# Sliding-window attention maxima taken over 64 queries of two heads at once, from separate copies of q and k in two-slot rings

## The chip, the cores and the metric

The kernel runs on one core of one Trainium2 chip. The metric is the device time of one execution in microseconds (us); shorter is better. TensorE (PE) does the matmuls and loads its stationary operands through a side path (PEld); VectorE (DVE), ScalarE (ACT) and GpSimd (POOL) work beside it; SyncE (SP) issues every DMA transfer, in the order of its queue.

## The reference

Two branches read the same x (2048 rows of 512) and are mixed by a gate per row. All arrays are float32.

```python
qkv = (x @ wqkv).reshape(1, 2048, 3, 32, 16)       # 32 heads of 16
scores = einsum("bhqd,bhkd->bhqk", q, k) * 16 ** -0.5
mask = (i - j >= 0) & (i - j < 256)                # causal, window of 256 keys
a = (softmax(where(mask, scores, -1e9)) @ v) @ wo
b = gelu(x @ w1 + b1) @ w2 + b2                    # 512 -> 1792 -> 512
g = sigmoid((x * gate_w).sum(-1))
out = g * a + (1 - g) * b
```

## The kernel before

Matrix products with weights are split into high and low parts and run as three matmuls each (`mm3`, L89 to L92). Rows are taken in four chunks of T = 512, each of four blocks of 128.

**The program in time.** `qkv(t)` for the four chunks comes first: x is transposed, q, k and v are made, and stored to DRAM (`SQ`, `SK`, `SV`). q and k are stored as two parts (high and low), 16 x 2 rows a head. Then attention runs over 8 groups of four heads, each of 16 blocks, so 128 steps `u`, with pieces of the dense branch (`mlp`, eight turns) between them; then `final`, the product with `wo`. One loop at the end of the function writes the order: at a step it emits, four times over, one matmul for maxima (`att_max`, eight blocks ahead, LEAD = 8), one for scores (`att_exp`), and dense work worth a quarter of STEP = 2296 ns. At every fourth step `att_pvs` multiplies the weights with v for a chunk.

**Maxima and scores.** `att_max` (L382 to L403) multiplies 128 queries of one head with up to 384 keys into a PSUM tile `sm` (three buffers), and DVE adds a mask and takes the row maximum in one instruction (L399), so a block of four heads is four matmuls and four DVE instructions. `att_rows` (L405) waits for four blocks, splits minus the maxima into two parts, transposes them on DVE (L414) and lets POOL copy them as rows into `qs` (`put`, L419). `att_exp` (L424) then gets scores less the maximum out of one matmul over 128 contraction rows; ACT takes the exponential and POOL zeroes the two triangles outside the window.

**Storage.** `qs` holds q for all 2048 queries, 96 rows of parts and 8 rows of maxima; `ks` holds k for all keys, the two heads of a pair interleaved by 64 columns and zeros or ones elsewhere (`clear_k`, L176). Both matmuls read the same two. `load_k` and `att_load` (L348 to L373) refill a chunk of both when its last reader of the group before is done; the third part of a head is the stored high part read once more.

**What sets the order.** PE, ACT, DVE and POOL run in the order in which the program emits their instructions. Work that comes later on other engines is put on a list by `after(ns, ...)` and emitted when a running count (`tick`) passes its due time. SP's queue is ordered by the framework's scheduler, and a transfer that waits holds back all that stand behind it.

**Buffers that the change touches.** Weights come through `raw` (three buffers; each load is split into two parts 10.5 us after it is due, and loads are 4 us apart, LAND and PACE). `h` has eight buffers, for q, k and v on their way to DRAM (L243, L264) and for the seven hidden tiles of an mlp turn. `pt` has 16 (PTS), two a step.

Of the kernel before, what the change touches and what calls it, by code (L numbers as in the profile page):

```python
# [18 lines left out]
T = 512  # L19
# [13 lines left out]
def gated_mix(ctx: ExitStack, tc: tile.TileContext, x, wqkv, wo, w1, b1, w2, b2, gate_w, out):  # L33
# [11 lines left out]
    def f32(ap):  # L45
# [6 lines left out]
    SQ = [dr.tile([H, 16, 2, T], F32, name=f"SQ{t}") for t in range(NT)]  # L52
    SK = dr.tile([H, 16, 2, S], F32, name="SK")
# [13 lines left out]
    mask = cp.tile([128, 384], BF16, name="mask")  # L67
    nc.gpsimd.memset(mask, 0.0)
    nc.gpsimd.affine_select(out=mask[:, 0:128], in_=mask[:, 0:128], pattern=[[1, 128]],
                            compare_op=ALU.is_ge, fill=NEG, base=-1, channel_multiplier=-1)  # L70
    nc.gpsimd.affine_select(out=mask[:, 256:384], in_=mask[:, 256:384], pattern=[[-1, 128]],
                            compare_op=ALU.is_ge, fill=NEG, base=0, channel_multiplier=1)
# [5 lines left out]
    for k in (0, 1):  # L78
        nc.gpsimd.affine_select(out=own[96:104], in_=own[96:104], pattern=[[-2, 4]], compare_op=ALU.not_equal,
                                fill=1.0, base=-k, channel_multiplier=1)  # L80
    nms = cp.tile([128, RB, 32], F32R, name="nm")
# [39 lines left out]
    def load_raw(key, early=False):  # L121
# [6 lines left out]
        if early and kind == "v":  # L128
            if i == 0:
                raws["v"] = f32(sb.tile([128, NC, 2, T], F32R, tag="xt", bufs=1, name="raw_v"))  # L130
            raw = raws["v"][:, i, 0]
        elif early:
            raw = sb.tile([128, 2, 320], F32, tag="pt", bufs=PTS, name=f"raw_{kind}{i}")
            raw = raw.rearrange("p a b -> p (a b)")[:, 0:T]
        else:
            raw = sb.tile([128, T], F32, tag="raw", bufs=3, name=f"raw_{kind}{i}")
# [32 lines left out]
    ks = cp.tile([128, 2, 2 * S], F32R, name="ks")  # L169
# [6 lines left out]
    def clear_k(i):  # L176

        pr, n = divmod(i, 4)
        for s in range(2):
            v = of_head(ks[:, pr, n * 1024:(n + 1) * 1024], s)  # L180
            nc.scalar.activation(v, nil.unsqueeze(2).unsqueeze(3).broadcast_to([128, 4, 2, 64]), AF.Identity,
                                 bias=own[:, 2 * pr + s:2 * pr + s + 1])

    xts, xrs = {}, {}

    def load_xr(t):
        for b in range(NB):
            xrs[t, b] = sb.tile([128, D], F32, tag=("tmp", "raw")[b // 3], bufs=3, name=f"xr{t}_{b}")
            nc.sync.dma_start(xrs[t, b], x[t * T + b * 128:t * T + (b + 1) * 128])

    def qkv_x(t, b):

        if b == 0:
            if t < NT - 1:
                v = (ks[:, 0], ks[:, 1], qs.rearrange("p a c -> p (a c)"))[t]
# [38 lines left out]
    def qkv_qk(t, j):  # L234
# [8 lines left out]
        e = sb.tile([128, 2, T], F32R, tag="h", bufs=8, name=f"qke{t}_{j}")  # L243
# [6 lines left out]
        def lo():  # L250
            nc.vector.tensor_sub(e[:, 1 - h], p, f32(e[:, h]))  # L251
            nc.sync.dma_start(dst[8 * i:8 * i + 8].rearrange("h d s c -> (h d) s c"), f32(e))
# [3 lines left out]
    def qkv_v(t, b):  # L256
# [7 lines left out]
        vx = f32(sb.tile([128, 2, T], F32R, tag="h", bufs=8, name=f"vx{t}_{b}"))  # L264
# [19 lines left out]
    def qkv(t):  # L284
# [17 lines left out]
        for n, (kind, j) in enumerate(pieces):  # L302
# [17 lines left out]
            if t == 2 and n in (1, 3, 5, 7):  # L320
                clear_k(4 + n // 2)
            if t == 2 and n in (2, 4):
                load_k(0, n // 2 - 1, slice(0, 1))
            if t == 2 and n in (9, 10):
                load_k(0, n - 9, slice(1, 2))
# [22 lines left out]
    def load_k(g_, c, prs):  # L348
# [3 lines left out]
        for pr in range(prs.start, prs.stop):  # L352
            for s in range(2):
                src = SK[4 * g_ + 2 * pr + s]
                for r, n, part in ((32 * s, 32, src.rearrange("d u c -> (d u) c")), (64 + 16 * s, 16, src[:, 0])):
                    v = f32(ks[r:r + n, pr])
                    k0, m = (c * T, NB) if s == 0 else (c * T - 64, NB) if c else (64, NB - 1)
                    to = v[:, 2 * k0 + 64:2 * k0 + 64 + 256 * m] if s else v[:, 2 * k0:2 * k0 + 256 * m]
                    to = to.rearrange("r (n x) -> r n x", x=256)
                    to = to[:, :, 0:128] if s else to[:, :, 64:192]  # L360
                    nc.sync.dma_start(to, part[:, k0:k0 + 128 * m].rearrange("r (n x) -> r n x", x=128))
                    if s and c == 0:
                        nc.sync.dma_start(v[:, 0:64], part[:, 0:64])
                    if s and c == NT - 1:
                        nc.sync.dma_start(v[:, 2 * S - 64:2 * S], part[:, S - 64:S])

    def att_load(g_, c, q_only=False):
        need(("qk", c, g_ // 2))
        if not q_only:
            load_k(g_, c, slice(0, 2))  # L370
        src, to = SQ[c][4 * g_:4 * g_ + 4], f32(qs[:, :, c * T:(c + 1) * T])
        nc.sync.dma_start(to[0:64], src.rearrange("(a s) d u c -> (s d u) a c", a=2))
        nc.sync.dma_start(to[64:96], src[:, :, 1].rearrange("(a s) d c -> (s d) a c", a=2))  # L373
# [11 lines left out]
    def att_max(g_, b, i):  # L385

        if b % RB == 0 and (g_, b // RB) not in Ms:
            Ms[g_, b // RB] = sb.tile([128, RB, 4], F32, tag="M", bufs=2, name=f"M{g_}_{b}")
        M = Ms[g_, b // RB]
        k0 = max(b - 2, 0) * 128  # L390
        w = (b + 1) * 128 - k0
        pr, s = divmod(i, 2)
        p = ps.tile([128, 384], F32, tag="sm", bufs=3, name=f"sm{g_}_{b}_{i}")
        nc.tensor.matmul(p[:, :w], qs[0:96, pr, b * 128:(b + 1) * 128], of_head(ks[0:96, pr, 2 * k0:2 * (k0 + w)], s),  # L394
                         start=True, stop=True)
        junk = sb.tile([128, 384], BF16, tag="jm", bufs=1, name=f"jm{g_}_{b}_{i}")

        def red():
            nc.vector.tensor_tensor_reduce(junk[:, :w], p[:, :w], mask[:, 384 - w:384], 1.0, -3e38,  # L399
                                           ALU.add, ALU.max, M[:, b % RB, i:i + 1])  # L400
# [4 lines left out]
    def att_rows(g_, rb):  # L405
# [3 lines left out]
        nm = nms[:, :, 0:8].rearrange("p b (i k) -> p k b i", k=2)  # L409
# [3 lines left out]
        tt = sb.tile([128, RB, 32], F32, tag="tt", bufs=1, name=f"tt{g_}_{rb}")  # L413
        nc.vector.transpose(tt.rearrange("p b c -> p (b c)"), f32(nms).rearrange("p b c -> p (b c)"))  # L414

        def put(i):
            dst = qs[96:104, :, rb * RB * 128:(rb + 1) * RB * 128]
            dst = dst.rearrange("r s (b i j) -> r s b i j", b=RB, i=4)[:, :, :, i]
            nc.gpsimd.tensor_copy(dst, tt[32 * i:32 * i + 8].unsqueeze(1).broadcast_to([8, 2, RB, 32]))  # L419
# [5 lines left out]
    def att_exp(g_, kb, i):  # L425
# [9 lines left out]
        nc.tensor.matmul(p[:, :w], ks[:, pr, 2 * k0:2 * k0 + 128], qs[:, pr, k0:k0 + w],  # L435
# [99 lines left out]
    def load_o(t, cs=range(NC)):  # L535

        if ("o", t) not in xts:
# [3 lines left out]
            else:  # L541
                xts["o", t] = [sb.tile([128, 2, T], F32R, tag="h", bufs=8, name=f"ot{t}_{c}") for c in range(NC)]
        ot = xts["o", t]
        for c in cs:
            need(("o", t, c))
            if t == 0:
                raw = sb.tile([128, T], F32, tag=("x1", "raw")[c % 2], bufs=2 + c % 2, name=f"or{t}_{c}")
# [60 lines left out]
    def mlp(n):  # L608
# [6 lines left out]
        for i in range(HF):  # L615
# [7 lines left out]
            h = sb.tile([128, 2, T], F32R, tag="h", bufs=8, name=f"h{t}_{f}")  # L623
# [48 lines left out]
    def load_y(t):  # L672

        need(*[("y", 1, t, b) for b in range(NB)])
        for i in range(NB // 2):
            v = f32(ks[:, i, 2 * t * T:2 * (t + 1) * T]).rearrange("p (j f) -> p j f", j=2)
# [67 lines left out]
    chunks = [divmod(i, NT) for i in range(NG * NT)]  # L744
    fill(START - AHEAD)
    need(("v", NT - 2, NB - 1))
    att_load(*chunks.pop(0), True), att_load(*chunks.pop(0), True)
    fill(AHEAD)
    for u in range(-LEAD, NU):
# [15 lines left out]
        if m % NB == LPOS and m > 0 and chunks:  # L765
            att_load(*chunks.pop(0))
        if u % NB == 0 and u >= 0:
            att_load_v(*divmod(u // NB, NT))
        if u >= NU - NKB + NB and u % NB == 1:
            load_y((u % NKB) // NB - 1)  # L770
# [8 lines left out]
LPOS = 0  # L779
LASTN = 2  # L780
WARM = (7, 3)
RB = 4
NKB = S // 128
PTS = 16
# [36 lines left out]
```

## Time and profile before

| quantity | value |
|---|---|
| time, median of 3 runs | 769.8 us (769.8 to 769.93) |
| the profiled execution's own time | 769.51 us |
| its span, first to last instruction | 767.8 us |
| granted TensorE clock | 1.00 |
| PE busy | 748.8 us, 98% |
| DVE, ACT, POOL busy | 534.1, 432.6, 385.9 us |
| moved by DMA | 137.81 MB, DMA engines busy 59.4% on the main queue |

The span lies 1.7 us under the profiled time. Shares over the whole span mix stages: the first 130 us are projections, then come attention and the dense branch together, and the last 50 us are the dense tail. A matmul's printed duration holds the time to fill and drain the array, which overlaps with its neighbours; the distance between the starts of two neighbours is what it takes from PE.

### The profile page before, as it was taken

The page shows a single profiled execution, that of the slowest core. Times are in us where ns is not written, and L with a number is a line of the kernel's source. Part 1 is how long each engine was busy: PE and PEld are TensorE (multiplying, and loading weights), DVE is VectorE, ACT ScalarE, POOL GpSimd, SP SyncE. Part 2 cuts the span into 40 slices and gives each one's busy share as a digit, 9 for nine tenths or more (in the row PEclk, how much of TensorE's full clock was granted, in tenths as well). Part 3 has the DMA queues.
Part 4 walks back from the last instruction along what each step waited for, and adds up shares of the span by engine and source line. Part 5 has one row for each costly group of instructions (what it writes and reads, how often), then busy time and mean ns, then how long its engine had stood idle before and what let it go on. Part 6 is the DMA issues. An engine that isn't in the chain of part 4 may idle for free.

```text
span 767.8 us, 18330 instructions
## 1 busy us (share of the span) xinstructions
PE 748.8 (98%) x6102; PEld 614.3 (80%) x6102; DVE 534.1 (70%) x1548; ACT 432.6 (56%) x945; POOL 385.9 (50%) x1125
## 2 busy tenths in 40 slices
PE   8999999988999999999999999999999999999998
PEld 6888888866888888788877877888888788878786
DVE  4532332889669868976897798679878886893553
ACT  4434433358458646754885587448646763785641
POOL 2200000018666765766567677658765775777200
PEclk9999999999999999999999999999999999999999
DMA  9986856765643565575345756653575474436583
GB/s 299 358 296 203 319 182 219 252 195 166 179 119 73 181 196 138 142 209 151 95 114 156 212 163 193 185 126 94 172 206 158 107 214 125 132 107 200 171 261 110
DMA packets 136558, 137.81 MB, mean 179 GB/s; under 512 B 53264, under 2 KB 88592, under 8 KB 136464
## 3 DMA queue, kind: packets, MB, share of 16 engines
q1 hardware_dynamic: 136464, 136.64, 59.4%
q8 instruction: 49, 0.80, 0.4%
q14 instruction: 45, 0.37, 0.2%
HBM read 82.58 MB, written 54.00 MB: 178 GB/s over the span
## 4 chain that ended last, share of the span: by engine, by line
PE 84%; DVE 8%; issue 3%; ACT 3%; DMA 1%; SPq 1%; POOL 0%; DVEq 0%; POOLq 0%; ACTq 0%
PE sm L394 10%; PE st L435 8%; PE pv_sm L472 7%; PE y L90 7%; PE y L91 6%; PE y L92 6%; PE u L90 5%; PE u L91 5%; PE u L92 5%; PE qk L92 4%; DVE jm L399 4%; PE qk L90 4%; PE qk L91 4%; PE a L90 2%; PE v L92 2%
## 5 line engine op out<-in xcount | busy, mean ns | idle before, releaser
L399 DVE CUSTOM_DVE_ANT_0 jm<-sm,mask 128x384 bf16<-128x384 f32 (+2 forms) x512 | 269.6, 527 | 66.8 <-PE sm L394 38.8
L450 ACT ACTIVATE pt<-st 128x320 f32<-128x320 f32 (+4 forms) x512 | 206.1, 421 | 134.1 <-PE st L435 129.4
L441 POOL TENSOR_SCALAR_AFFINE_SELECT pt<-pt 64x128 f32<-64x128 f32 x512 | 176.5, 345 | 184.8 <-ACT pt L450 166.1
L394 PE MATMUL sm<-ks,qs 96*128 96x384 f32 (+2 forms) x512 | 171.7, 338 | 10.7 <-DVE M L399 9.0
L435 PE MATMUL st<-qs,ks 128*128 128x320 f32 (+4 forms) x512 | 155.0, 305 | 0.7 <-ACT pt L450 0.7
L444 POOL TENSOR_SCALAR_AFFINE_SELECT pt<-pt 64x128 f32<-64x128 f32 x448 | 154.7, 345 | 0.0
L394 PEld LDWEIGHTS sm<-ks,qs 96*128 96x128 f32 x512 | 96.2, 188 | 44.1 <-DVE M L399 21.1
L435 PEld LDWEIGHTS st<-qs,ks 128*128 128x128 f32 x512 | 97.3, 190 | 18.3 <-ACT pt L450 1.1
L90 PE MATMUL y<-w,h 128*128 128x512 f32 x224 | 90.1, 402 | 0.0
L91 PE MATMUL y<-w,h 128*128 128x512 f32 x224 | 88.4, 395 | 0.0
L92 PE MATMUL y<-w,h 128*128 128x512 f32 x224 | 87.8, 392 | 0.0
L419 POOL CAST qs<-tt 8x256 fp32r<-8x256 f32 x128 | 62.3, 487 | 47.2 <-PE u L92 37.9
L90 PE MATMUL u<-mx,w 128*128 128x512 f32 x196 | 80.4, 410 | 0.0
L91 PE MATMUL u<-mx,w 128*128 128x512 f32 x196 | 77.3, 395 | 0.0
L92 PE MATMUL u<-mx,w 128*128 128x512 f32 x196 | 76.8, 392 | 0.0
L472 PE MATMUL pv_st<-pt,vbuf 64*32 64x320 f32 (+4 forms) x1408 | 73.1, 346 | 0.8 <-POOL pt L441 0.8
L472 PE MATMUL pv_sm<-pt,vbuf 64*32 64x320 f32 (+4 forms) x1408 | 73.4, 346 | 0.1
L472 PEld LDWEIGHTS pv_sm<-pt,vbuf 64*32 64x32 f32 x1408 | 49.9, 106 | 19.9 <-issue 2.1
L251 DVE TENSOR_TENSOR qke<-qk,qke 128x512 fp32r<-128x512 f32 x32 | 22.1, 690 | 48.9 <-ACT qke L248 40.5
L248 ACT ACTIVATE qke<-qk 128x512 fp32r<-128x512 f32 x32 | 19.1, 598 | 56.0 <-PE qk L92 37.1
L92 PEld LDWEIGHTS y<-w,h 128*128 128x128 f32 x224 | 42.1, 188 | 9.7
L496 DVE TENSOR_TENSOR nd<-nd,pv_sm 128x512 f32<-128x512 f32 x32 | 21.9, 684 | 39.0 <-ACT nd L493 38.8
(124 smaller groups left out, 1337.6 us busy)
## 6 DMA issues: line engine op xcount, KB each, us to landing
mx<-XT SPq DMA_DIRECT2D x24, 512.0 KB
SQ<-qke SPq DMA_DIRECT2D x16, 512.0 KB
SK<-qke SPq DMA_DIRECT2D x16, 512.0 KB
qs<-SQ SPq DMA_DIRECT2D x32, 256.0 KB
ND<-nd SPq DMA_DIRECT2D x32, 256.0 KB
ks<-SK SPq DMA_DIRECT2D x112, 64.0 KB
raw_w<-in_B_w_dram SPq DMA_DIRECT2D x28, 256.0 KB
SV<-vx SPq DMA_DIRECT2D x16, 272.0 KB
```

Source lines behind the costliest of these rows:

```text
L90: nc.tensor.matmul(p, lh, rh, start=first, stop=False)
L91: nc.tensor.matmul(p, lh, rl, start=False, stop=False)
L92: nc.tensor.matmul(p, ll, rh, start=False, stop=last)
L251: nc.vector.tensor_sub(e[:, 1 - h], p, f32(e[:, h]))
L394: nc.tensor.matmul(p[:, :w], qs[0:96, pr, b * 128:(b + 1) * 128], of_head(ks[0:96, pr, 2 * k0:2 * (k0 + w)], s), start=True, stop=True)
L399: nc.vector.tensor_tensor_reduce(junk[:, :w], p[:, :w], mask[:, 384 - w:384], 1.0, -3e38, ALU.add, ALU.max, M[:, b % RB, i:i + 1])
L419: nc.gpsimd.tensor_copy(dst, tt[32 * i:32 * i + 8].unsqueeze(1).broadcast_to([8, 2, RB, 32]))
L435: nc.tensor.matmul(p[:, :w], ks[:, pr, 2 * k0:2 * k0 + 128], qs[:, pr, k0:k0 + w], start=True, stop=True)
L441: nc.gpsimd.affine_select(out=v[:, :, 0:64], in_=v[:, :, 0:64], pattern=[[0, 2], [1, 64]], compare_op=ALU.is_ge, fill=0.0, base=0, channel ...
L444: nc.gpsimd.affine_select(out=v[:, :, W:W + 64], in_=v[:, :, W:W + 64], pattern=[[0, 2], [-1, 64]], compare_op=ALU.is_ge, fill=0.0, base=- ...
L450: nc.scalar.activation(pt[:, pr, :w], p[:, :w], AF.Exp, scale=SCALE)
L472: nc.tensor.matmul(pv[r // 64][32 * i:32 * i + 32, q - c * T:e - c * T], vts[g_, b // NB][r:r + 64, v:v + 32], rhs(r), start=start, stop=s ...
```

## The change

`att_max` now takes 64 queries of both heads of a pair at once. The queries lie in a new tile `qd`, block-diagonal: head 0's 64 queries in rows 0 to 47, head 1's in rows 48 to 95, zeros elsewhere. The keys lie in a new tile `kd`, both heads' parts one above the other, without interleaving. 64 queries see at most 320 keys. A block is still four matmuls and four DVE instructions, over 320 columns for 384. `qd`, `kd` and `ks` are rings of two chunk slots; `qs` stays whole. The rows of minus the maxima move to rows 0 to 3 and 64 to 67 of `qs`, four partitions of 512 elements where there were eight of 256. q and k are stored with three parts a head, the third by a transfer of its own. `h` goes from 8 buffers to 7, `raw` from 3 to 2, `pt` from 16 to 14; weight loads before 150 us of the program's count are staged in `pt`.

```diff
-    SQ = [dr.tile([H, 16, 2, T], F32, name=f"SQ{t}") for t in range(NT)]
-    SK = dr.tile([H, 16, 2, S], F32, name="SK")
+    SQ = [dr.tile([H, 16, 3, T], F32, name=f"SQ{t}") for t in range(NT)]
+    SK = dr.tile([H, 16, 3, S], F32, name="SK")
...
-    nms = cp.tile([128, RB, 32], F32R, name="nm")
+    nms = cp.tile([128, 2 * RB, 32], F32R, name="nm")
...
-    ks = cp.tile([128, 2, 2 * S], F32R, name="ks")
+    ks = cp.tile([128, 2, 2, 2 * T], F32R, name="ks")
+    qd = cp.tile([128, 2, 2, 2 * T], F32R, name="qd")
+    kd = cp.tile([128, 2, 2, W + T], F32R, name="kd")
...
-            nc.sync.dma_start(dst[8 * i:8 * i + 8].rearrange("h d s c -> (h d) s c"), f32(e))
+            to = dst[8 * i:8 * i + 8].rearrange("h d s c -> (h d) s c")
+            nc.sync.dma_start(to[:, 0:2], f32(e))
+            nc.sync.dma_start(to[:, 2], f32(e[:, h]))
...
+    def load_ks(g_, c):
+        need(("qk", c, NC + g_ // 2))
+        src = parts(SK, g_, slice(c * T, (c + 1) * T))
+        for pr in range(2):
+            for s in range(2):
+                v = f32(ks[64 * s + 4:64 * s + 52, pr, slot(g_, c)]).rearrange("r (n u j) -> r n u j", u=4, j=64)
+                w = src[s, :, pr].rearrange("r (n u j) -> r n u j", u=2, j=64)
+                if s:
+                    nc.sync.dma_start(v[:, :, 0], w[:, :, 0])
+                    nc.sync.dma_start(v[:, :, 3], w[:, :, 1])
+                else:
+                    nc.sync.dma_start(v[:, :, 1:3], w)
+    def load_kd(g_, c):
+        need(("qk", c, NC + g_ // 2))
+        k0 = max(c * T - W, 0)
+        src = SK[4 * g_:4 * g_ + 4, :, :, k0:(c + 1) * T].rearrange("(a s) d u c -> (s d u) a c", s=2)
+        nc.sync.dma_start(f32(kd[0:96, :, slot(g_, c), k0 - c * T + W:]), src)
+    def load_qd(g_, c):
...
+                v = f32(qd[48 * s:48 * s + 48, pr, slot(g_, c)]).rearrange("r (n s j) -> r n s j", s=2, j=64)[:, :, s]
+                nc.sync.dma_start(v, src[s, :, pr].rearrange("r (n j) -> r n j", j=64))
+    def load_qs(g_, c):
...
+            nc.sync.dma_start(f32(qs[64 * s + 4:64 * s + 52, :, c * T:(c + 1) * T]), src[s])
...
-        k0 = max(b - 2, 0) * 128
-        w = (b + 1) * 128 - k0
-        nc.tensor.matmul(p[:, :w], qs[0:96, pr, b * 128:(b + 1) * 128], of_head(ks[0:96, pr, 2 * k0:2 * (k0 + w)], s),
+        hb, pr = divmod(i, 2)
+        w = min(64 * (2 * b + hb + 1), W + 64)
+        k1 = 64 * (j + 1) + W
+        nc.tensor.matmul(p[:, :w], qd[0:96, pr, n, 128 * j:128 * (j + 1)], kd[0:96, pr, n, k1 - w:k1],
...
+            r = 64 * (i // 2)
+            dst = qs[r:r + 4, :, rb * RB * 128:(rb + 1) * RB * 128]
+            nc.gpsimd.tensor_copy(dst, tt[32 * i:32 * i + 4].unsqueeze(1).broadcast_to([4, 2, 2 * RB, 32]))
...
-        if m % NB == LPOS and m > 0 and chunks:
-            att_load(*chunks.pop(0))
+        if m in range(1, NT + 1):
+            load_qs(0, m - 1)
+        if m % NB == 0 and 0 < m < NU - NB:
+            load_qd(*divmod(m // NB + 1, NT)), load_kd(*divmod(m // NB + 1, NT))
+        if u % NB == 1 and NB < u < NU - NB:
+            load_ks(*divmod(u // NB + 1, NT))
+        if u % NB == 2 and NB < u < NU - 3 * NB:
+            load_qs(*divmod(u // NB + 3, NT))
```

On PE the instructions stand in the same order as before, one for one. What moves is SP's queue. At the end of the third chunk of the first group of heads SP's rows before were these (`nd` is a chunk's result of attention, `vbuf` holds v):

```order
L361 DMA ks<-SK 32x4x128
L361 DMA ks<-SK 16x4x128 x2
L372 DMA qs<-SQ_72 64x2x512
L373 DMA qs<-SQ_72 32x2x512
L380 DMA vbuf<-SV_78 128x4x34
L382 DMA vbuf<-SV_78 64x4x34
L497 DMA ND_0_95<-nd_2_2529 128x512
L382 DMA vbuf<-SV_78 64x4x34
```

And with the change, at the same place:

```order
L395 DMA qd<-SQ_72 48x8x64 x3
L529 DMA ND_0_95<-nd_2_2565 128x512
L395 DMA qd<-SQ_72 48x8x64
L387 DMA kd<-SK 96x2x768
L408 DMA vbuf<-SV_78 128x4x34
L410 DMA vbuf<-SV_78 64x4x34 x2
L381 DMA ks<-SK 48x4x128
L378 DMA ks<-SK 48x4x64
L379 DMA ks<-SK 48x4x64
L381 DMA ks<-SK 48x4x128
L378 DMA ks<-SK 48x4x64
L379 DMA ks<-SK 48x4x64
```

The four transfers of `qd` and the one of `kd` now stand at the head of a chunk, around the store of `nd`; v follows, then the six of `ks`, and behind these rows the two of `qs`.

On POOL the copies of the maxima (`CAST`) keep their place between the two triangle selections of a block. Before and after, at the second chunk's first block:

```order
L444 AFFINE_SELECT pt_4_0_1886<-pt_4_0_1886 64x2x64
L419 CAST qs<-tt_2_1896 8x2x4x32 x3
L441 AFFINE_SELECT pt_4_1_1909<-pt_4_1_1909 64x2x64
```

```order
L476 AFFINE_SELECT pt_4_0_1919<-pt_4_0_1919 64x2x64
L450 CAST qs<-tt_2_1930 4x2x8x32 x3
L473 AFFINE_SELECT pt_4_1_1943<-pt_4_1_1943 64x2x64
```

Only their shape changed.

124 lines of the change are left out of this document (62 added, 62 removed).

## The prediction

> **What bounds the kernel now.** First the page's busy times and the granted clock, then the matmuls in time, then what PE waits for, then the stretches.
>
> ```profile
> PE 748.8 (98%) x6102; PEld 614.3 (80%) x6102; DVE 534.1 (70%) x1548; ACT 432.6 (56%) x945; POOL 385.9 (50%) x1125
> PEclk9999999999999999999999999999999999999999
> ```
>
> PE is busy for 98% at full clock, so in most of the span each column that a matmul does not stream is time. The groups by shape give durations; a piece of PE's timeline (start, duration) gives the price of a column:
>
> ```profile
> L394 PE MATMUL sm<-ks,qs 96*128 96x384 f32 x448 | 155.5, 350 | 10.7 <-DVE M L399 9.0 <-DVE nd L496 1.2
> L394 PE MATMUL sm<-ks,qs 96*128 96x256 f32 x32 | 9.0, 282 | 0.0
> L394 PE MATMUL sm<-ks,qs 96*128 96x128 f32 x32 | 7.3, 228 | 0.0
> L435 PE MATMUL st<-qs,ks 128*128 128x320 f32 x448 | 139.9, 314 | 0.7 <-ACT pt L450 0.7
> ...
> 208.10 0.40 PE L90 MATMUL y<-w,h 128*128 128x512 f32 x1
> 208.33 0.39 PE L91 MATMUL y<-w,h 128*128 128x512 f32 x1
> 208.56 0.39 PE L92 MATMUL y<-w,h 128*128 128x512 f32 x1
> 208.79 0.28 PE L394 MATMUL sm<-ks,qs 96*128 96x256 f32 x1
> 208.91 0.31 PE L435 MATMUL st<-qs,ks 128*128 128x320 f32 x1
> 209.06 0.28 PE L394 MATMUL sm<-ks,qs 96*128 96x256 f32 x1
> ```
>
> Starts are 0.23 us apart behind 512 columns, 0.12 behind 256, 0.15 behind 320: 0.45 to 0.47 ns a column, the weight loads hidden. Next, everything that PE stood idle for, with the longest single wait last in each row:
>
> ```profile
> PE sm L394 <- DVE M L399: 9.0, 17, 1.2
> PE warm0.0_177 L281 <- POOL idle L49: 1.3, 1, 1.3
> PE sm L394 <- DVE nd L496: 1.2, 3, 0.5
> PE pv_st L472 <- POOL pt L441: 0.8, 1, 0.8
> PE pv_sm L472 <- DVE M L399: 0.8, 3, 0.3
> PE st L435 <- ACT pt L450: 0.7, 1, 0.7
> PE qk L90 <- ACT qk L145: 0.7, 1, 0.7
> PE u L90 <- ACT sqh L572: 0.3, 1, 0.3
> ```
>
> No transfer is in this list: PE waits for no DMA. What it does wait for is DVE, which is late in emptying the three `sm` buffers. The stretches say where (length, then PE, PEld, DVE, ACT and POOL busy, clock, DMA share, GB/s):
>
> ```profile
> 20.00:40.00 20.00, 20.00 (x97) 16.53 (x97) 9.81 (x18) 9.47 (x20) 4.71 (x7) 1.00 0.95 341
> ...
> 160.00:190.00 30.00, 24.78 (x171) 18.23 (x170) 26.34 (x74) 21.95 (x46) 17.85 (x43) 1.00 0.62 202
> 190.00:700.00 510.00, 502.68 (x4749) 414.92 (x4749) 408.66 (x1262) 319.60 (x718) 343.06 (x1005) 1.00 0.55 152
> ```
>
> At the start of attention (160 to 190) PE loses 5.2 us and DVE is 88% busy; over the 510 us behind it PE loses 7.3 us.
>
> **The maxima on PE.** The count of matmuls stays. Of the 512, 448 go from 384 to 320 columns; of the 32 of a group's second block, half go from 256 to 192; of the 32 of its first, half go from 128 to 64. That is 480 matmuls of 64 columns less. At 0.45 ns a column, 29 ns each, the sum is **13.9 us**. Bounds: the mean durations 350 and 314 differ by 36 ns, 17 us; the gap of 0.03 us between 256 and 320 columns in the timeline, read at its rounding (20 ns), 10 us. The order on PE does not move and the stationary operand stays 96 by 128, so no load is added. I take 13.9, since the spacing is what PE pays.
>
> **The maxima on DVE.**
>
> ```profile
> L399 DVE CUSTOM_DVE_ANT_0 jm<-sm,mask 128x384 bf16<-128x384 f32 x448 | 247.1, 551 | 54.3 <-PE sm L394 29.4 <-PE st L435 0.3
> L399 DVE CUSTOM_DVE_ANT_0 jm<-sm,mask 128x256 bf16<-128x256 f32 x32 | 13.6, 424 | 8.6 <-PE sm L394 7.1
> L414 DVE STREAM_TRANSPOSE tt<-nm 128x128 f32<-128x128 f32 x32 | 10.0, 311 | 4.0 <-DVE nm L411 0.5 <-POOL pt L444 0.5
> L419 POOL CAST qs<-tt 8x256 fp32r<-8x256 f32 x128 | 62.3, 487 | 47.2 <-PE u L92 37.9 <-DVE tt L414 2.6
> ```
>
> 551 less 424 over 128 columns is 0.99 ns a column, so 64 columns are 64 ns, and 480 of them 30.5 us of DVE. The transpose of twice the columns costs between nothing and another 311 ns; at the same 0.99 ns a column 127 ns, 4.1 us in 32 (at most 10). DVE thus gives back 26 us, most of it while PE is busy anyway. What counts is the backlog: a block asks 4 x 64 ns less of DVE (0.03 us of that spent on transposes) and 4 x 29 ns less of PE, so DVE gains 0.11 us a block on PE. If DVE sets the pace in half of the 128 blocks (the gelu halves), that is 7 us; PE's visible waits on DVE (9.0 + 1.2) are the ceiling, 0 the floor. I take **4.5 us** off, a little under the middle, since part of the backlog comes from DVE standing behind `nd`, which the change leaves.
>
> **POOL.** The 128 copies keep their bytes but run over 512 elements in 4 partitions where there were 256 in 8: between 487 ns and twice that; if a POOL instruction goes by elements, nearer the upper end, 0 to 62 us in all and up to 2 us a chunk. POOL is busy 343 of 510 us in attention, and no row above is a wait for these copies. Scores first need them two steps later, and what stands behind them on POOL is the selections of a chunk just begun, which `pv` reads a chunk later. Cover gone, 2 us in each of 32 chunks would be exposed. I cost it at nothing.
>
> **Transfers.**
>
> ```profile
> DMA packets 136558, 137.81 MB, mean 179 GB/s; under 512 B 53264, under 2 KB 88592, under 8 KB 136464
> q1 hardware_dynamic: 136464, 136.64, 59.4%
> ...
> 300.67 2.73 SPq L361 DMA_DIRECT2D ks<-SK  x5
> ...
> 311.91 1.29 SPq L382 DMA_DIRECT2D vbuf<-SV  x2
> ...
> 331.42 1.72 SPq L382 DMA_DIRECT2D vbuf<-SV  x2
> ...
> SPq L361 <- PE st L435: 65.7, 53, 6.1
> SPq L137 <- DVE w L149: 24.6, 16, 4.1
> ```
>
> Projections: the third part of q and k adds 32 stores of 256 KB, 8.4 MB; at 341 GB/s for a share of 0.95, the rate of the stretch from 20 to 40 us, 23 us of all engines over some 150 us. PE was 100% busy in that stretch with DMA at 0.95, so that close a queue does not reach it. The x rows are the reader nearest by; in SP's queue of the first chunk they stand no later than before. Nothing.
>
> Attention: a chunk reads `qd` 384 KB, `kd` 576 KB (96 rows, two pairs, 768 columns), `ks` and `qs` 384 KB each; before, only the last two. That is 0.98 MB more, 2.7 us of all engines by bytes at the rate above. By packets: `qd` in rows of 64 columns has 1536, `ks` 1152 for 768, `kd` 192, 2112 more; at the mean packet of 53 ns (59.4% of 16 x 767.8 us over 136464), 7.0 us. A chunk lasts 19.5 us (the two `vbuf` rows), so the share goes from 0.55 to between 0.69 and 0.91. The Trainium skill's page "DMA: Bandwidth & Descriptors", section Specifications, speaks against the change: transfers in pieces under 512 B do a read-modify-write. Were the 256-byte rows of `qd` and half of `ks`, 576 KB, to count twice, a chunk would take an estimated 1.6 us more than by bytes, still within the bound by packets; no row of this run isolates it.
>
> Lateness: a chunk has 16 issues (4 `qd`, 1 `kd`, 3 v, 6 `ks`, 2 `qs`). Five `ks` took 2.73 us, 0.55 each, so 8.8 us; then 1.8 MB to land, 5.3 us by bytes. Together 14 of 19.5 us, and the ring slot is free as the chunk begins, so SP loses most of the 65.7 us for which it waited on scores. I cost it at nothing; the cover is 5 us, and the longest hold of SP before was 6.1.
>
> Smaller pools: with two `raw` buffers a load must wait for the one two before it, due 8 us earlier, which DVE frees some 12 us after its time (LAND plus the split). So a load starts 4 us late and has about 6.5 us to land before ACT wants it. Where SP is held, ACT, and behind it the exponentials, stand for a few us, at 14 paced loads at most. Between 0 and 6 us; **1.5 us** on. With 7 `h` and 14 `pt` the next use follows the last reader in the program's order, and I add nothing.
>
> Sum against the profiled execution: 769.5 - 13.9 - 4.5 + 1.5 = 752.6. Its time lies 0.3 us under the median, so **753 us**.
>
> **Rivals.**
>
> 1. *The rings starve PE (slower).* `ks` is loaded behind `qd`, `kd` and v, and at a chunk's first score PE stands until it lands. Against it: 14 of 19.5 us, and nothing waited for DMA before. For it: the share may reach 0.91, and one hold of SP eats the cover. It decides once issue and landing pass 19.5 us; at 1 us over in each of 28 chunks 753 + 28 = 781 us.
> 2. *The staging of weights.* ACT waits at most loads through `raw`, the full 6 us in place of 1.5: 757, and with the DVE relief gone too, 762.
> 3. *DVE gives nothing back.* The transposes stand in front of maxima and cost the full 311 ns, and the backlog behind `nd` stays: 769.5 - 13.9 + 1.5, 757.
> 4. *The copies on POOL come late.* 2 us a chunk are exposed at the scores: 753 + 64, or 785 at half. For it only the doubled length.
> 5. *The columns saved are not PE's time.* DVE sets the pace throughout and gives less than it saves: no change, 769. Against it: PE loses 7.3 of 510 us.
>
> **How the numbers follow.** Forecast 0.64; rival 1 0.09, 2 0.11, 3 0.10, 4 0.03, 5 0.03. The likeliest is 753; with its own bounds (10 to 17 on PE, 0 to 10 on DVE) it spans 744 to 761. The range takes in rivals 2 and 3 as well and leaves out 1, 4 and 5, 0.15 in all: 745 to 763. A measurement can tell about 0.2% from no change. Faster 0.85 (forecast, 2, 3), within 0.2% 0.03 (5), slower 0.12 (1, 4).
>
> **What would show it.** `sm` matmuls of 320 columns at 314 ns, starts 0.15 us apart, x448; the DVE instruction at 487 ns; PE's waits on `M` under 9.0 us; PE still at 97% or more. PE's list without DMA and without `qs` copies. A row `sm <- DMA kd` or `st <- DMA ks` of many us would be rival 1, `ACT w <- DMA raw_w` rival 2, `st <- POOL qs` rival 4. DVE at 508 us, POOL up by as much as 62 us and the DMA share at 0.69 to 0.91 would bear out the bounds.

## The result, and the profile after

The changed kernel takes **805.7 us** (median of 4 runs, 802.71 to 806.79) against 769.8 before: a ratio of 1.046, interval 1.0432 to 1.0489. It is 36 us slower; 753 was predicted. The profiled execution took 806.2 us, its span is 804.5. Of all the executions used below, one, of the version with three slots of `ks`, ran in a slower state (892.66 us at a granted clock of 0.754) and is in no ratio.

The page of the changed kernel, busy times, then the transfers:

```profile
PE 755.9 (94%) x6102; PEld 616.2 (77%) x6102; DVE 510.1 (63%) x1548; ACT 432.8 (54%) x941; POOL 422.7 (53%) x1129
...
DMA packets 208494, 176.09 MB, mean 219 GB/s; under 512 B 126480, under 2 KB 150288, under 8 KB 208400
...
q1 hardware_dynamic: 208400, 174.91, 78.6%
```

PE is no longer busy for 98% of the span, and though it streams 480 x 64 columns less, its busy time went up by 7 us: the matmuls themselves took longer, at a mean granted clock of 0.975 for 1.00. Packets rose by half. What PE waited for (sum, times, longest), then what SP's queue waited for:

```profile
PE st L467 <- DMA ks<-SK: 19.6, 14, 3.7
PE sm L424 <- DMA kd<-SK: 10.3, 4, 6.5
PE sm L424 <- DVE M L429: 2.4, 7, 0.5
```

```profile
SPq L529 <- DVE nd L528: 43.3, 15, 4.8
...
SPq L378 <- DMA kd<-SK: 18.0, 15, 2.3
...
SPq L549 <- DMA RD<-den: 14.6, 6, 6.0
```

The list that held no transfer before is now led by two. SP, which had waited for scores, now waits most for what it has to store (`nd`, made on DVE) and for its own earlier transfers to land: 15 times a `ks` of one head stood until `kd` had landed. The wait for the `sm` buffers, the only real one before, shrank from 9.0 to 2.4 us. The stretches of attention (length, then PE, PEld, DVE, ACT and POOL busy, clock, DMA share, GB/s):

```profile
160.00:190.00 30.00, 22.46 (x121) 18.38 (x127) 23.57 (x68) 21.01 (x46) 15.52 (x32) 0.89 0.79 200
190.00:700.00 510.00, 477.88 (x4514) 389.95 (x4499) 361.66 (x1199) 295.29 (x662) 350.52 (x945) 0.97 0.79 198
```

Over the 510 us PE now loses 32 (7.3 before), at a clock of 0.97 for 1.00. The DMA share went from 0.55 to 0.79, but the rate from 152 to 198 GB/s: share grew by 44%, bytes by 30%.

**The first stop.** The chain of work that ended last, PE's timeline, and the stretches around it, 5 us each:

```profile
153.02 8.74 DMA SK<-qke
161.77 8.35 DMA kd<-SK
```

```profile
170.25 0.60 PE L424 MATMUL sm<-kd,qd 96*128 96x320 f32 x1 [6.53 <-DMA kd<-SK]
```

```profile
160.00:165.00 5.00, 3.58 (x16) 2.39 (x14) 3.95 (x12) 2.83 (x5) 0.00 (x0) 1.00 1.20 262
165.00:170.00 5.00, 0.00 (x0) 0.00 (x0) 1.10 (x3) 1.78 (x3) 0.00 (x0) 0.72 1.07 249
170.00:175.00 5.00, 4.75 (x15) 4.09 (x16) 3.96 (x13) 2.38 (x6) 1.39 (x4) 0.60 1.00 174
175.00:180.00 5.00, 4.62 (x24) 3.76 (x22) 4.86 (x13) 4.95 (x11) 4.70 (x9) 1.00 0.02 7
```

The store of k takes 8.7 us, `kd`, which reads it, another 8.4, with the DMA engines full; PE stands for 6.5 us. Behind the stop the matmuls run at a granted clock of 0.60 over 5 us. So the stop costs more than its own length.

**A stop at the scores.** SP's timeline ahead of one, PE's waits, and the stretches of 4 us:

```profile
441.54 0.57 SPq L395 DMA_DIRECT2D qd<-SQ  x1
442.56 0.62 SPq L549 DMA_DIRECT2D num<-ND  x1
446.11 0.61 SPq L549 DMA_DIRECT2D rb<-RD  x1
446.81 0.41 SPq L529 DMA_DIRECT2D ND<-nd  x1
447.27 1.94 SPq L395 DMA_DIRECT2D qd<-SQ  x3
449.25 1.18 SPq L387 DMA_DIRECT2D kd<-SK  x1
...
453.89 0.43 SPq L381 DMA_DIRECT2D ks<-SK  x1
456.04 0.32 SPq L378 DMA_DIRECT2D ks<-SK  x1
...
457.86 0.44 SPq L379 DMA_DIRECT2D ks<-SK  x1
```

```profile
456.16 0.39 PE L424 MATMUL sm<-kd,qd 96*128 96x320 f32 x1 [0.85 <-DMA kd<-SK]
459.72 0.61 PE L467 MATMUL st<-qs,ks 128*128 128x320 f32 x1 [3.17 <-DMA ks<-SK]
```

```profile
452.00:456.00 4.00, 3.12 (x14) 1.80 (x12) 3.57 (x13) 2.29 (x6) 1.74 (x6) 1.00 1.00 233
456.00:460.00 4.00, 0.67 (x2) 0.50 (x3) 0.33 (x2) 0.69 (x1) 0.00 (x0) 0.67 0.80 229
460.00:464.00 4.00, 4.00 (x21) 3.09 (x28) 3.13 (x11) 1.93 (x5) 1.26 (x3) 0.50 0.92 241
```

From the store of `nd` to the score that waited are 12.9 us, much like the 14 us of the prediction. One of the four `qd` went out at 441.5. The rest of the row starts only with the store at 446.8, 9.7 us before PE wants `ks` (459.72 less 3.17): the loads of the normalisation (`num`, `rb`) and the store, all ahead in the queue, held it. It is the same at all seven stops of over 1 us for `ks` (1.06 to 3.72 us): the store of `nd` went out 8.7 to 13.3 us before PE wanted `ks`. The DMA engines are at 1.00 with 233 GB/s, not the 341 that the estimate used.

**The clock.** At 460 to 464 the granted clock is 0.50. Two more stretches of 4 us, the first at the end of a stop of 2.01 us of the changed kernel, the second behind one of 3.76 us in a run below (narrow maxima with the old transfers):

```profile
668.00:672.00 4.00, 3.41 (x10) 2.90 (x11) 0.92 (x3) 0.88 (x2) 0.81 (x4) 0.62 0.92 215
```

```profile
332.00:336.00 4.00, 4.00 (x13) 3.52 (x12) 2.47 (x9) 1.31 (x3) 1.49 (x6) 0.50 0.18 41
```

The second has the DMA engines nearly idle (0.18), while the clock was 1.00 at 160 to 165 and at 452 to 456 with shares of 1.20 and 1.00: the low clock goes with the stop and not with the traffic. In the changed kernel the clock falls below 0.9 in eight places, seven of them at a stop of PE of 2.01 us or more, one at two of 1.06 and 0.82 us with one matmul between; four single stops of 1.06 to 1.65 us left it at 1.00. The Trainium skill's page "TensorE: Matmul & The Clock Gate", section "HAM oscillation — how this bites in real kernels", gives the rule that PE should have no idle gap of more than about 3.4 us, behind which it is throttled to half its clock. The trace agrees on the half (0.50) but not on the length: here a gap of 2.01 us was enough.

The groups by shape:

```profile
L429 DVE CUSTOM_DVE_ANT_0 jm<-sm,mask 128x320 bf16<-128x320 f32 x448 | 217.0, 484 | 68.6 <-PE sm L424 46.5
...
L424 PE MATMUL sm<-kd,qd 96*128 96x320 f32 x448 | 142.6, 321 | 14.0 <-DMA kd<-SK 10.3 <-DVE M L429 2.4 <-DVE nd L528 0.7
...
L450 POOL CAST qs<-tt 4x512 fp32r<-4x512 f32 x128 | 90.2, 705 | 46.2 <-DVE tt L444 38.9
L444 DVE STREAM_TRANSPOSE tt<-nm 128x256 f32<-128x256 f32 x32 | 14.3, 445 | 3.3
```

The engines' own costs came out as forecast: the maximum 484 ns (487), the matmul 321 (314), the transpose 445 (311 + 127), the copy 705, between its bounds of 487 and 974.

### The profile page after: what moved, and what is told of

Same layout as the page of the kernel before. It is cut to its first block, busy times and chain, and to the rows that moved or that the text cites. A ratio compares the mean times of both kernels' runs of the same rounds, so it can differ in the third digit from the quotient of the medians.

```text
span 804.5 us, 18387 instructions
## 1 busy us (share of the span) xinstructions
PE 755.9 (94%) x6102; PEld 616.2 (77%) x6102; DVE 510.1 (63%) x1548; ACT 432.8 (54%) x941; POOL 422.7 (53%) x1129
## 2 busy tenths in 40 slices
DMA packets 208494, 176.09 MB, mean 219 GB/s; under 512 B 126480, under 2 KB 150288, under 8 KB 208400
## 3 DMA queue, kind: packets, MB, share of 16 engines
q1 hardware_dynamic: 208400, 174.91, 78.6%
## 4 chain that ended last, share of the span: by engine, by line
PE 68%; DMA 20%; DVE 5%; issue 2%; SPq 2%; POOL 1%; ACT 1%; DVEq 0%; POOLq 0%
PE pv_sm L504 7%; PE st L467 6%; PE sm L424 6%; DMA ks<-SK 6%; PE u L93 5%; PE u L95 4%; PE u L94 4%; DMA kd<-SK 4%; PE y L93 4%; PE qk L93 4%; PE qk L95 4%; PE qk L94 4%; PE y L94 4%; PE y L95 4%; DMA qd<-SQ 2%
## 5 line engine op out<-in xcount | busy, mean ns | idle before, releaser
L429 DVE CUSTOM_DVE_ANT_0 jm<-sm,mask 128x320 bf16<-128x320 f32 (+4 forms) x512 | 237.5, 464 | 91.5 <-PE sm L424 67.1
L473 POOL TENSOR_SCALAR_AFFINE_SELECT pt<-pt 64x128 f32<-64x128 f32 x512 | 186.7, 365 | 178.3 <-ACT pt L482 157.1
L467 PE MATMUL st<-qs,ks 128*128 128x320 f32 (+4 forms) x512 | 159.5, 315 | 21.3 <-DMA ks<-SK 19.6
L424 PE MATMUL sm<-kd,qd 96*128 96x320 f32 (+4 forms) x512 | 158.2, 311 | 14.5 <-DMA kd<-SK 10.3
L476 POOL TENSOR_SCALAR_AFFINE_SELECT pt<-pt 64x128 f32<-64x128 f32 x448 | 152.4, 340 | 0.0
L424 PEld LDWEIGHTS sm<-kd,qd 96*128 96x128 f32 x512 | 98.0, 191 | 43.1 <-DVE M L429 13.5
L450 POOL CAST qs<-tt 4x512 fp32r<-4x512 f32 x128 | 90.2, 705 | 46.2 <-DVE tt L444 38.9
L95 PE MATMUL y<-w,h 128*128 128x512 f32 x224 | 89.7, 400 | 1.7 <-DVE h L619 1.7
L93 PE MATMUL y<-w,h 128*128 128x512 f32 x224 | 91.1, 407 | 0.0
L94 PE MATMUL y<-w,h 128*128 128x512 f32 x224 | 89.8, 401 | 0.0
L504 PE MATMUL pv_sm<-pt,vbuf 64*32 64x320 f32 (+4 forms) x1408 | 77.5, 358 | 2.8 <-DVE M L429 2.4
L504 PE MATMUL pv_st<-pt,vbuf 64*32 64x320 f32 (+4 forms) x1408 | 77.0, 358 | 0.6 <-POOL pt L473 0.6
L504 PEld LDWEIGHTS pv_st<-pt,vbuf 64*32 64x32 f32 x1408 | 49.0, 110 | 0.9 <-POOL pt L473 0.9
```

The lines of the kernel that those rows point to most:

```text
L93: nc.tensor.matmul(p, lh, rh, start=first, stop=False)
L94: nc.tensor.matmul(p, lh, rl, start=False, stop=False)
L95: nc.tensor.matmul(p, ll, rh, start=False, stop=last)
L424: nc.tensor.matmul(p[:, :w], qd[0:96, pr, n, 128 * j:128 * (j + 1)], kd[0:96, pr, n, k1 - w:k1], start=True, stop=True)
L450: nc.gpsimd.tensor_copy(dst, tt[32 * i:32 * i + 4].unsqueeze(1).broadcast_to([4, 2, 2 * RB, 32]))
L467: nc.tensor.matmul(p[:, :w], ks[:, pr, slot(g_, kb // NB), at:at + 128], qs[:, pr, k0:k0 + w], start=True, stop=True)
```

## Experiments

The kernel before took 770.1 to 770.7 us (medians) beside these runs. Ratios are to it.

### The gain alone: narrow maxima with the old transfers

The kernel before, with its maxima over as many columns as the change takes, from neighbouring columns of `ks` (they mix the two heads, so the maxima are not the right ones).

```diff
-        w = (b + 1) * 128 - k0
+        w = min((b + 1) * 128 - k0 - (64 if b < 2 and i % 2 else 0), W + 64)
...
-        ... of_head(ks[0:96, pr, 2 * k0:2 * (k0 + w)], s),
+        ... ks[0:96, pr, 2 * k0:2 * k0 + w],
```

> The kernel before with maxima over 320 columns (192 and 64 where the change has them), all its transfers as before; the columns are those of both heads interleaved, so the maxima are not the reference's. If the gain that was forecast for PE and DVE is real and only the transfers spoil it: 750 to 757 us (13.9 off on PE, 0 to 6 off DVE's backlog). If the narrower maxima give nothing by themselves: 768 to 771.

Measured 758.35 us, ratio 0.9837 (0.9807 to 0.9868). PE's waits and the stretch of attention:

```profile
PE sm L394 <- DVE M L399: 6.3, 12, 1.3
```

```profile
190.00:700.00 510.00, 498.85 (x4869) 412.88 (x4868) 377.19 (x1260) 322.26 (x725) 350.79 (x1026) 0.99 0.57 156
```

The gain is real: 12.3 us beside the runs of before on its chip (770.65), though the time is a little over the 750 to 757 that were expected. PE's busy time fell by 12.9 us, its wait for DVE by 2.7, and one new wait, 3.8 us for `h`, stands against that. From here to the changed kernel are **47.4 us**, which is what the rest of the change costs (the kernel before took 770.65 us beside the one and 769.8 beside the other). Span less PE's busy time is 21.2 us here and 48.6 with the change, so 27.4 of the 47.4 are standing still; the other 20.0 are the same matmuls taking longer (735.9 us of busy time against 755.9). The mean clock, 0.995 against 0.975, accounts for some 15 of these 20 (735.9 x 0.995 / 0.975 = 751.0); what the other 5 are is not traced.

### Is it the order of the queue?

Both runs ask for the transfers earlier, so that they stand ahead of the store of `nd`: `qd`, `kd` and `ks`, or `ks` alone. The edit for `ks`:

```diff
-        if u % NB == 1 and NB < u < NU - NB:
-            load_ks(*divmod(u // NB + 1, NT))
+        if u % NB == 3 and 0 < u < NU - 2 * NB:
+            load_ks(*divmod(u // NB + 2, NT))
```

> The changed kernel with the loads of qd, kd and ks emitted at the last step of the chunk that frees their slot, so that in SP's queue they stand ahead of the store of nd. Queue theory (they were late because the store of nd, which waits for the chunk's own result, stood ahead of them): PE's waits for kd and ks go from 30 us to under 8, the clock back to 0.99 or more, 755 to 768 us. Bytes theory (the DMA engines cannot land them in time however early they are issued): PE still waits over 20 us for them, 790 us or more.

> The changed kernel with only the loads of ks emitted earlier; qd and kd stay behind the store of nd. Queue theory: the waits for ks (19.6 us) go, those for kd (10.3) stay or grow, 775 to 790 us. Bytes theory: no more than 5 us from the changed kernel, 800 us or more.

Measured 820.84 us (ratio 1.0648, 1.059 to 1.0706) for all three and 800.27 (1.038, 1.0321 to 1.0439) for `ks` alone. PE's, SP's and DVE's waits with all three earlier:

```profile
PE sm L424 <- DVE M L429: 39.7, 17, 7.3
PE y L95 <- DVE h L619: 8.2, 2, 7.6
```

```profile
SPq L539 <- DMA ND<-nd: 25.0, 12, 4.3
...
SPq L554 <- DVE num L553: 19.2, 5, 7.3
```

```profile
DVE num L553 <- DMA rb<-RD: 56.6, 13, 8.6
```

PE hardly waits for `kd` or `ks` any more (1.0 us in all), and the kernel is 15 us slower than the changed one: now the loads of the normalisation come last, DVE, which runs in order, stands 56.6 us before them, and PE stands behind DVE. With `ks` alone earlier the time is 5 us under the changed kernel's: no wait of a score for `ks` is left, but those of the maxima for `kd` went from 10.3 to 15.2 us. The theory that the queue's order alone is the cause falls: in both runs what was then last was late.

### Is it the amount?

The changed kernel with the same transfers in the same places, but from the second group of heads on only a quarter of the columns of `qd` and `ks` and 128 of the 768 of `kd` are loaded; the rest keeps older values, so the results are not right.

```diff
+        if g_:
+            k0 = (c + 1) * T - 128
```

> The changed kernel with the same transfers in the same queue order, but from the second group of heads on qd, kd and ks get only a quarter of their columns (128 of 768 for kd), the rest keeping old data. Queue theory: it stays slow, 785 us or more, with PE waiting 15 us or more for ks and kd. Bytes theory: the DMA share in attention falls from 0.79 to about 0.6 and the time to 770 us or less.

Measured 764.03 us, ratio 0.991 (0.9882 to 0.9937): 41.7 us of the 47.4 are back. The first group was not cut, and PE's only wait for a transfer is the first stop:

```profile
PE sm L429 <- DMA kd<-SK: 6.6, 1, 6.6
```

```profile
190.00:700.00 510.00, 500.27 (x4917) 412.20 (x4901) 387.83 (x1270) 322.69 (x726) 382.53 (x1032) 1.00 0.57 157
```

That stop is about the 5.7 us that remain to 758.35. POOL's longer copies, the third store and the smaller pools are all in this run, so together they cost no more than these 5.7 us.

### Bytes or packets?

One transfer at a time: `kd` cut to 128 columns (fewer bytes, as many packets), `qd` to a quarter (fewer of both), and `qd` in rows of 2 KB for pieces of 256 B (as many bytes, fewer packets; the queries then do not lie block-diagonal). The edit of the last:

```diff
-                v = f32(qd[48 * s:48 * s + 48, pr, slot(g_, c)]).rearrange("r (n s j) -> r n s j", s=2, j=64)[:, :, s]
-                nc.sync.dma_start(v, src[s, :, pr].rearrange("r (n j) -> r n j", j=64))
+                v = f32(qd[48 * s:48 * s + 48, pr, slot(g_, c)])[:, s * T:(s + 1) * T]
+                nc.sync.dma_start(v, src[s, :, pr])
```

> The changed kernel, but from the second group on kd gets only the last 128 of its 768 columns (480 KB a chunk less, in rows of 512 B for 3 KB, their number unchanged); the maxima then use stale keys. All else as changed. The run with a quarter of qd, kd and ks took 41.7 us off 805.7. If the time of the DMA engines goes by bytes, 480 of the 1056 KB which that run saved are saved here: 787 us. If it goes by the number of packets (small pieces, 192 of 192 still there), nothing is saved: 803 to 807. If it is a threshold (the share of busy DMA engines must fall to about 0.7 and then nothing is late), all of it comes back: 764 to 770.

> The changed kernel, but from the second group on qd gets a quarter of its columns (288 KB a chunk less, 1152 fewer packets of 256 B); the maxima then use stale queries. By bytes 288 of 1056 KB: 794 us. By number of packets 1152 of the 2016 saved by the run that cut all three: 782 us. By threshold: it lies between the other two cuts, 770 to 800.

> The changed kernel, but qd is loaded in rows of 2 KB for pieces of 256 B: the same 384 KB a chunk in 192 packets for 1536, in the same four transfers at the same places; the queries then do not lie block-diagonal, and the maxima are of wrong sums. If only bytes count: 802 to 807. If small packets cost beyond their bytes (the cut of qd gave 30 us for 288 KB, the cut of kd 21 us for 480 KB): by those two, 1.7 us per MB leaves 16 us for the 32 thousand packets of the cut of qd, so 43 thousand fewer give some 20 us: 780 to 790.

Measured 784.58 (ratio 1.0169, 1.0127 to 1.0212), 775.77 (1.0072, 1.0048 to 1.0096) and 781.82 us (1.0149, 1.0103 to 1.0196). The rows of 2 KB, page and stretch:

```profile
DMA packets 165487, 176.09 MB, mean 226 GB/s; under 512 B 77328, under 2 KB 101136, under 8 KB 165392
```

```profile
190.00:700.00 510.00, 490.58 (x4667) 402.67 (x4673) 381.36 (x1257) 315.87 (x706) 371.19 (x989) 0.99 0.78 203
```

Not a byte less, 43 thousand packets fewer: 23.9 us faster. `kd`, with no packet less and 12.4 MB fewer, gave 21.2. So both count, and `qd`, the smaller transfer, costs more than `kd`: the cut of 288 KB a chunk of it gave 30.0 us, that of 480 KB of `kd` 21.2. By these two prices (1.7 us per MB, 0.56 us per thousand packets) the cut of `qd` (8.25 MB, 32.3 thousand packets) should give 32 us; it gave 30. The share of 0.78 is that of the changed kernel (0.79), but over a shorter span: 78.7% of 780.3 us against 78.6% of 804.5 are 18 us less for the engines, so a mean share does not tell the one from the other. In the changed kernel's trace a packet of 256 B took 18 ns (median) and one of 2 KB 84, so eight small ones take 144. The prediction cited the Trainium skill's page "DMA: Bandwidth & Descriptors", section Specifications, on pieces under 512 B, and estimated 1.6 us a chunk from it for `qd` and half of `ks`; the rows of 2 KB gave 23.9 us of the kernel's time over 32 chunks, 0.75 each, for `qd`. That small pieces cost extra agrees; whether a read-modify-write is behind it no run shows.

### The other parts alone: the third store, the pools

Each added to the kernel before and nothing else.

```diff
+            nc.sync.dma_start(SX[t][8 * j:8 * j + 8].rearrange("h d c -> (h d) c"), f32(e[:, h]))
```

> The kernel before with the third store alone: each q and k piece of the projections stores its high part a second time, 32 more transfers of 256 KB, to a DRAM array that nothing reads. By the prediction it costs nothing: 769 to 771. By the rival (the queue and the DMA engines at a share of 0.95 at the end of the projections delay the first loads of attention): 3 to 7 us, 773 to 777, with the stretch from 120 to 190 us slower and the rest the same.

> The kernel before with the smaller pools of the change alone: h 7 buffers for 8, raw 2 for 3, pt 14 for 16, and weights before 150 us of the program's count staged in pt. By the prediction's term (a weight load waits for the one two before it): 1.5 us, at most 6: 770 to 776, with rows of ACT or DVE behind raw_w. By the rival that the pools cost nothing: 769.5 to 771.5. Had they a part in the 36 us of the change, well above 776.

Measured 770.5 us (ratio 1.0005, 0.9995 to 1.0015) and 771.02 (1.0016, 1.0003 to 1.0028). The store costs nothing, though it lifts the DMA share at 120 to 160 us from 0.68 to 0.86; the pools cost about 1 us.

### A cheaper form: maxima from the high parts

Any number near the row's maximum will do, since it cancels in the quotient of the softmax. So `qd` and `kd` need the high parts only, 32 rows for 96. First the matmul over these 32 rows, then over 96 of which 64 are zero.

```diff
-        nc.sync.dma_start(f32(kd[0:96, :, slot(g_, c), k0 - c * T + W:]), src)
+        nc.sync.dma_start(f32(kd[0:32, :, slot(g_, c), k0 - c * T + W:]), src)
...
-        nc.tensor.matmul(p[:, :w], qd[0:96, pr, n, ...], kd[0:96, pr, n, k1 - w:k1],
+        nc.tensor.matmul(p[:, :w], qd[0:32, pr, n, ...], kd[0:32, pr, n, k1 - w:k1],
```

> The changed kernel, but the maxima are taken from the high parts alone: qd and kd are 32 rows (16 a head) for 96, in every group, so a chunk reads 128 KB of qd for 384 and 192 KB of kd for 576. The subtracted maximum then differs a little from the true one, which cancels in the quotient of the softmax. If bytes and packets of the two make PE wait, this brings back most of it: by the threshold 757 to 765, in proportion to bytes (640 of 1056 KB) 780. PE's waits for kd under 5 us. If the queue's order or the ring's slots were the cause, 795 to 806.

> The changed kernel with the maxima from the high parts alone, as in the run that came out at 928 us, but over 96 contraction rows, 64 of them zero: qd and kd load 32 rows (640 KB a chunk less, 1152 packets fewer) and TensorE's matmul keeps its shape. If the 928 us were the 32-row shape beside 128-row ones (0.34 us from start to start for 0.15), PE now starts 0.15 us apart and the time is 757 to 766, below both kernels. By the cuts of kd (21 us for 480 KB a chunk) and qd (30 us for 288 KB and 1152 packets) together there is room for all 41.7 us that the cut of all three took. If the high parts or the transfers into 32 partitions were what cost, it stays above 800.

Measured **928.2 us** (ratio 1.2055, 1.2026 to 1.2083) over 32 rows and 773.24 (1.0039, 1.0022 to 1.0055) over 96. PE's timeline with 32 rows, then with 96:

```profile
330.25 0.41 PE L424 MATMUL sm<-kd,qd 32*128 32x320 f32 x1
330.59 0.41 PE L467 MATMUL st<-qs,ks 128*128 128x320 f32 x1
330.93 0.41 PE L424 MATMUL sm<-kd,qd 32*128 32x320 f32 x1
```

```profile
329.49 0.31 PE L425 MATMUL sm<-kd,qd 96*128 96x320 f32 x1
329.64 0.31 PE L468 MATMUL st<-qs,ks 128*128 128x320 f32 x1
```

A matmul over 32 rows next to one over 128 starts 0.34 us after it and holds up the next by as much, where two of 96 and 128 rows start 0.15 us apart. 0.19 us on all 1024 matmuls of maxima and scores would be 195 us, more than the 155 by which the 32 rows lost to the 96. The Trainium skill's page "TensorEngine Tiling (Array Packing)", section "Key Properties", says that a change of the tiling mode drains TensorE; these starts fit it and give the price, though no run shows that 32 rows beside 128 are such a change. Padding with zeros costs nothing that shows in the starts and takes 155 us off.

The 773.2 us missed the 757 to 766 that were expected. With 156.16 MB and 171630 packets it takes back 32.5 of the 47.4 us; by the prices above 54 were to be had, so these do not add up once the worst is gone. Six waits for `ks` are left, 6.9 us.

### What is left

`ks` asked for two steps earlier, `ks` cut to a quarter, and a version meant to win: both pairs' keys in the same columns of `kd` (64 rows), and a third slot of `ks` in the room that gives, loaded a chunk ahead.

```diff
-    ks = cp.tile([128, 2, 2, 2 * T], F32R, name="ks")
-    kd = cp.tile([128, 2, 2, W + T], F32R, name="kd")
+    ks = cp.tile([128, 2, 3, 2 * T], F32R, name="ks")
+    kd = cp.tile([128, 2, W + T], F32R, name="kd")
```

> The kernel with the maxima from the high parts over 96 rows (773.2 us), with ks asked for two steps earlier, at the end of a chunk. There six waits for ks summed to 6.9 us of TensorE. If ks is late only since it stands last in the queue, and the DMA engines have room at a share of 0.64, the waits go and the time is 763 to 768, below the kernel before. If the lateness moves to qd, kd or the transfers of the normalisation, as it did at a share of 0.79: 771 to 780.

> The same kernel (773.2 us), with ks in its old place but a quarter of its columns from the second group on (288 KB a chunk less, 864 fewer packets); scores then use stale keys. The bytes are then about those of the run with three cuts (764.0), and the first group reads less. If what is left is the transfers alone: 756 to 762, the time of the narrow maxima with the old transfers (758.4). If something else in the change costs the rest (the copies on POOL, the pools, the clock): 765 to 772.

> A version meant to beat the kernel before. Maxima from the high parts over 96 rows, as in the run of 773.2 us, with the two pairs' keys one above the other in the same columns of kd (64 rows, half the columns), and the room used for a third slot of ks: a chunk of ks is asked for a whole chunk earlier (19.5 us) into a slot that has long been free; pt has 13 buffers for 14. Bytes and packets stay. If lateness of what stands last in the queue is all that is left, a chunk of slack ends the waits for ks: 758 to 766. If the transfers of the normalisation and of qd are late in its place, as when ks was asked for two steps earlier (776.7): 771 to 780.

Measured 776.73 (ratio 1.0086, 1.0067 to 1.0104), 767.18 (0.9961, 0.9947 to 0.9974) and 772.6 us (1.0015, 0.9998 to 1.0032). Earlier is a little worse here (776.73 for 773.24). Cutting takes off 6 more, though not all: PE still stands 4.5 us for `ks`, three times. With the third slot no transfer of q or k stands long before PE, but DVE waits:

```profile
PE sm L426 <- DVE M L431: 5.8, 10, 1.2
PE pv_sm L506 <- DVE M L431: 5.7, 3, 3.0
```

```profile
DVE den L545 <- DMA den<-ND: 10.2, 8, 3.6
DVE num L555 <- DMA rb<-RD: 7.5, 5, 2.5
```

So the last try lets DVE come to the normalisation later, in that version and in the changed kernel:

```diff
-        after(6000, rcp), after(10500, back), after(17000, mul)
+        x = 1.0 if c == NC - 1 else 1.5
+        after(6000 * x, rcp), after(10500 * x, back), after(17000 * x, mul)
```

> The kernel with three slots of ks (772.6 us), and the steps of the normalisation (reciprocal, reading back, product) emitted half as late again after their loads: 9, 15.75 and 25.5 us for 6, 10.5 and 17, except in the last two groups. There DVE stood 17.7 us for den and rb and PE waited for DVE. If these late transfers, met by an engine that runs in order, are what is left: DVE's rows for den and rb go, and the time is 758 to 766. If not: 770 to 774.

> The changed kernel (805.7 us) with the same later normalisation and nothing else. DVE stood there 33 us for den and rb, 24.2 and 8.8, off which a part reached PE. If the way through DVE carries a good part of the loss: 785 to 797. If PE's own waits for ks and kd (31 us) carry it: 800 to 808, with these waits as before.

Measured 779.88 (ratio 1.0122, 1.009 to 1.0154) and 806.05 us (1.0455, 1.042 to 1.049). In the changed kernel it does nothing for the time, though DVE's wait for `den` fell from 24.2 to 10.8 us: PE's own waits for `ks` and `kd`, 30.8 us before and 30.7 now, carry its loss. In the other it adds waits, most of all at `nd`:

```profile
PE sm L426 <- DVE nd L530: 18.7, 9, 4.4
```

No version that does the whole computation came under the kernel before; the one with three slots of `ks` cannot be told from it.

## Why the prediction was wrong

| part of the prediction | forecast | shown by | measured |
|---|---|---|---|
| maxima on PE and DVE | -18.4 us | narrow maxima alone (transposes as before) | -12.3 |
| third store | 0 | store alone | 0.3, interval with 0 |
| smaller pools | +1.5 | pools alone | about +1 |
| POOL's copies | 0 | run with the three cuts | under 6 with all the rest |
| transfers of attention | 0 | three cuts, and narrow alone | +42 of 47 |

**The step that failed** is "Together 14 of 19.5 us [...] I cost it at nothing; the cover is 5 us". Its 14 us was a fair length for the row of transfers: 12.9 us from the store of `nd` to the score at the stop shown. Three things were wrong around it.

- *The room was not 19.5 us.* The count ran from the start of a chunk, as if SP were free then. At the stop shown, all but one `qd` of the row started 9.7 us before PE wanted `ks`, behind `rb` and `nd`, since SP keeps its order; at the seven longest stops for `ks` it was 8.7 to 13.3 us. The store of `nd` had been shown as a row of SP's queue, and then only the transfers of the loads were counted. `ks` has no whole chunk in any case, for it is emitted at a chunk's second step.
- *The rate was that of another stage.* 341 GB/s stood in a stretch of the projections; ahead of the stop the engines are at 1.00 with 233. The bound by packets, 7.0 us a chunk, was nearer, and the share of 0.79 lies inside the 0.69 to 0.91 of the sum. But no wait was worked out from it, while the engines stood at 1.00 and above just before each stop shown.
- *A stop was priced at its own length.* Of the 47.4 us, 20.0 are longer matmuls, some 15 of them by the mean clock.

**Rival 1** was the right story, with a chance of 0.09 and a price of 28 us (1 us in each of 28 chunks). Standing still came to 27.4 us more, but that the two agree is luck: PE's list has 18 stops of up to 6.5 us for `kd` and `ks`, not 28 of 1 us. The clock, which it left out, and the smaller gain make up most of the rest to 806. What spoke for it was in the rows that were quoted: 53264 packets under 512 B before and 1536 pieces of 256 B more a chunk for `qd` alone, and SP waiting 65.7 us for scores to free what it loads into.

**The gain** has the right mechanism and was over-sized by 6 us. The columns gave 12.9 us of PE's busy time for 13.9; the relief of DVE's backlog, 4.5, was mis-sized: the wait for the `sm` buffers fell by 2.7 us, and one new wait of PE for `h`, 3.8 us, with the clock at 0.50 over 4 us behind it, stands against it. So the relief gave nothing net, which is rival 3's amount, though not for its reason: the transpose took 445 ns, not the 622 of that rival.

Right were DVE's and POOL's durations and totals (508 forecast for DVE, 510.1 measured; POOL up 37 of at most 62), the third store, the pools within a microsecond, and rivals 2, 4 and 5 not coming about: no row of ACT behind `raw_w`, a single wait of 0.9 us for POOL's copies, and the columns saved did come off PE.

**Open.** The version with 640 KB a chunk less still stands 15 us above the narrow maxima with the old transfers. Cutting `ks` takes 6 of them; for the other 9 the traces show DVE standing at the loads of the normalisation and at `nd`, and PE still at `ks`, but letting DVE come later made the version with three slots worse, so that cause is argued and not shown. That a stop lowers the clock is read from where the clock fell; no run made a stop of set length to measure it.

## What to carry to other kernels

Cost a new transfer by its deadline: from the moment SP reaches it, behind all that stands ahead and has to land, to the instruction that reads it, at the rate of rows of its own size. Count pieces of 256 B beside bytes, and look at the DMA share in the 5 us ahead of the need, since a mean of 0.79 hid stretches at 1.00. And before a matmul is made smaller to save a load, see what stands beside it: here padding 32 contraction rows with zeros to 96 left the starts 0.15 us apart, while 32 rows cost 155 us.

## What the runs showed of the hardware

- A matmul over 32 contraction rows between matmuls over 128: 0.34 us from start to start on both sides, 0.15 us for 96 rows beside 128.
- The granted clock behind a stop of PE: 0.60 over 5 us behind 6.53 us, 0.50 over 4 us behind 3.17 us, 0.62 over the 4 us at the end of 2.01 us; four single stops of 1.06 to 1.65 us left it at 1.00. In the kernel before, where no stop was over 1.3 us, it stayed at 1.00, also at 160 to 190 us, with PE busy for 24.78 of 30.
- The same 176.09 MB in 165 for 208 thousand packets: 23.9 us less at an unchanged DMA share (0.78 for 0.79); a packet of 256 B took 18 ns (median), one of 2 KB 84.
